# One weight load of a fused attention and mixture kernel, asked for in five pieces of its partitions instead of one

## The chip, the cores and the metric

The kernel runs on one core of one Trainium2 chip. A core has five engines that run side by side: TensorE (PE in the profile, its weight loads PEld), VectorE (DVE), ScalarE (ACT), GpSimd (POOL) and SyncE (SP), and sixteen DMA engines that move data between the main memory and the core's own memories. The metric is the time of one execution in microseconds (us), the median of several.

## What is computed

Sliding-window causal attention over 8 batches, 8 heads, 576 positions and 64 values per head, and behind it a soft mixture of 8 experts with 4 slots each:

```
scores = scale * q @ k.T          # where 0 <= row - column < 64
x = softmax(scores) @ v           # 4608 rows x 512
logits = x @ phi                  # 4608 x 32 slots
slot_input = softmax over rows of logits, transposed, @ x
slot_out[e] = relu(slot_input[e] @ w1[e]) @ w2[e]    # w1: 512 x 1024, w2: 1024 x 512
out = softmax over slots of logits @ slot_out        # 4608 x 512
```

All inputs and the output are float32. The kernel computes in float16; the loads issued from POOL convert on the way.

## The kernel before

The attention runs in 32 steps, one for each batch and pair of heads, in a software pipeline written out by hand: the order of the source is the order on each engine. Step `n` loads inputs for later steps, turns q and k, and does the scores, the maximum, the exponentials and the products of earlier steps. The logits and the slots' sums are folded in by batches. When the last batch is through, the slot inputs `sit` are known; then the experts' two layers run (`first`, L827, and `second`, L851), the result is gathered (`osb`, L880), and the rows of the output are made and written (`cps`, L898 to L905).

The weights are loaded all along from POOL's queue. `worder` lists the loads: the second half of the first matrix of the first weights, the other seven matrices, then the second weights. Of these the first six are whole matrices (`load_w2(e)`, e = 0 to 5), the last two come as halves of their columns: matrix 6 left, matrix 7 left, matrix 6 right, matrix 7 right. `load_w(n)` takes the next n of the list; where it is called (`wslot` and a few calls by hand) fixes their place among POOL's other work. A whole matrix of the second weights is 128 partitions of 8 rows of 512: each partition reads 16 KB in one run and writes 8 KB.

The sixth matrix of the second weights is the last load before POOL does `old_rows` (L515 to L526), which rearranges the sums of the earlier batches; its source order is

```python
    load_w(1)                  # the sixth matrix
    oldr, lgM = old_rows()
    load_w(2)                  # matrix 6 left, matrix 7 left
    ...
    load_w(2)                  # matrix 6 right, matrix 7 right
    scaled(nc.gpsimd, wO, five(olT), 0)      # L787, on POOL
```

The tensor `wO` that `scaled` writes goes into the slot inputs: DVE adds to it at L796 and builds `sit` at L804, which `first` multiplies with the first weights. Matrices six to eight of the second weights lie in a pool that takes the place of the staging buffers of q and k, which are closed by then.

The waits between engines are put in by the framework. For DMA requests from POOL it has eight completion semaphores, which it gives out in turn, in program order. A request that takes a semaphore again gets a wait, on POOL, for the request that had it before, unless POOL has already waited for that one. There are 68 requests from POOL in all. Outputs are requested from SP.

Of the kernel before, what the change touches and what calls it, by code (L numbers as in the profile page):

```python
# [20 lines left out]
def kernel(  # L21
# [10 lines left out]
    nc = tc.nc  # L32

    B, H, S, Dh = q.shape
    D, NSLOT = moe_phi.shape
    E, _, F = moe_w1.shape
# [22 lines left out]
    w2_t = [pwt.tile([128, NFC, D], FP16, name=f"w2_{e}") for e in range(NW2)]  # L59
# [4 lines left out]

    DH = D // 2

    def load_w2(e, d0=0, d1=D):
        src = moe_w2[e].rearrange("(p c) d -> p c d", p=128)
        nc.gpsimd.dma_start(out=w2_t[e][:, :, d0:d1], in_=src[:, :, d0:d1])

    att = ExitStack()
    apsum = ExitStack()
# [63 lines left out]
    for t_, src in reversed(tuple(zip(firsts, (q, k)))):  # L136
        nc.sync.dma_start(out=t_.rearrange("p (h e) -> p h e", h=2),
                          in_=src[0, 0:2].rearrange("h (p r) d -> p h (r d)", r=RQ))
# [370 lines left out]
    def old_rows():  # L509
# [10 lines left out]
        for r in range(4):  # L520
# [4 lines left out]
            if r:  # L525
                nc.gpsimd.tensor_tensor(out=ts[0], in0=ts[0], in1=ts[r], op=ALU.add)  # L526
        return ts[0], wq[:, 8 * w_:8 * w_ + 192]

    NH = 2
    worder = ([(load_w1, 0, 2, 4)] + [(load_w1, e) for e in range(1, E)] + [(load_w2, e) for e in range(E - NH)]  # L530
              + [(load_w2, e, DH * h, DH * h + DH) for h in range(2) for e in range(E - NH, E)])
    worder.reverse()

# [373 lines left out]
    for h in range(2):  # L907
        d0, d1 = DH * h, DH * h + DH
# [39 lines left out]
```

## Time and profile before

| | us |
|---|---|
| median of 3 runs | 192.03 |
| lowest, highest | 191.03, 193.9 |
| the profiled execution, its own time | 193.47 |
| its span, first to last instruction | 191.7 |

| engine | busy us | share of the span |
|---|---|---|
| PE | 152.3 | 79% |
| DVE | 138.4 | 72% |
| ACT | 131.2 | 68% |
| POOL | 130.9 | 68% |

The profile is one execution. The shares are averages over stages with different limits. The page's second part cuts the span into 40 slices of 4.8 us and gives the busy share of each engine in tenths; the sixteen DMA engines are at nine tenths in nearly all of them:

```profile
POOL 8798999997877969989796797966894840000000
DMA  6999999999999999999999999999999999999995
GB/s 145 188 180 184 198 189 182 175 220 178 175 215 181 174 208 183 174 205 194 179 205 195 179 192 212 203 216 215 217 214 212 205 197 164 229 347 367 408 431 250
```

The requests are in the page's sixth part (what, engine, operation, count, KB each, median us from issue to landing). The weights are 13 loads of a matrix or its size and 6 smaller ones:

```profile
w<-in_moe_w_dram POOLq DMA_DIRECT2D x13, 1024.0 KB, 17.7
vr<-in_v_dram POOLq DMA_DIRECT2D x16, 288.0 KB, 14.0
out_dram<-ob SPq DMA_DIRECT2D x2, 2304.0 KB, 7.4
ks<-in_k_dram POOLq DMA_DIRECT2D x15, 288.0 KB, 11.3
qs<-in_q_dram POOLq DMA_DIRECT2D x15, 288.0 KB, 11.8
out_dram<-oh SPq DMA_DIRECT2D x9, 384.0 KB, 4.8
w<-in_moe_w_dram POOLq DMA_DIRECT2D x6, 512.0 KB, 18.9
...
ks<-in_k_dram POOLq DMA_DIRECT2D x1, 144.0 KB, 5.0
qs<-in_q_dram POOLq DMA_DIRECT2D x1, 144.0 KB, 4.9
...
phi_sb<-in_moe_phi_dram POOLq DMA_DIRECT2D x1, 32.0 KB, 9.5
```

A time behind a request is the time until the whole of it has landed, so it holds the queue ahead of it. Waits are put down to the one that ended last.

### The profile page before, as it was taken

The page shows a single profiled execution, that of the slowest core. Times are in us where ns is not written, and L with a number is a line of the kernel's source. Part 1 is how long each engine was busy: PE and PEld are TensorE (multiplying, and loading weights), DVE is VectorE, ACT ScalarE, POOL GpSimd, SP SyncE. Part 2 cuts the span into 40 slices and gives each one's busy share as a digit, 9 for nine tenths or more (in the row PEclk, how much of TensorE's full clock was granted, in tenths as well). Part 3 has the DMA queues.
Part 4 walks back from the last instruction along what each step waited for, and adds up shares of the span by engine and source line. Part 5 has one row for each costly group of instructions (what it writes and reads, how often), then busy time and mean ns, then how long its engine had stood idle before and what let it go on. Part 6 is the DMA issues. An engine that isn't in the chain of part 4 may idle for free.

```text
span 191.7 us, 6887 instructions
## 1 busy us (share of the span) xinstructions
PE 152.3 (79%) x2886; PEld 114.2 (60%) x2886; DVE 138.4 (72%) x306; ACT 131.2 (68%) x255; POOL 130.9 (68%) x257
## 2 busy tenths in 40 slices
PE   5639878897979798988889888989889898689700
PEld 1428777785868587767678676857756245453100
DVE  5794898697888789877969877787675751668420
ACT  5933968878889589889778887969562141677500
POOL 8798999997877969989796797966894840000000
PEclk9855999999999999999999999999999699965555
DMA  6999999999999999999999999999999999999995
GB/s 145 188 180 184 198 189 182 175 220 178 175 215 181 174 208 183 174 205 194 179 205 195 179 192 212 203 216 215 217 214 212 205 197 164 229 347 367 408 431 250
DMA packets 61279, 41.14 MB, mean 215 GB/s; under 512 B 38720, under 2 KB 58944, under 8 KB 59328
## 3 DMA queue, kind: packets, MB, share of 16 engines
q0 software_dynamic: 56384, 30.68, 120.0%
q1 hardware_dynamic: 4864, 10.03, 14.1%
q8 instruction: 22, 0.36, 0.7%
q14 instruction: 9, 0.07, 0.1%
HBM read 61.93 MB, written 9.44 MB: 372 GB/s over the span
## 4 chain that ended last, share of the span: by engine, by line
DVE 30%; PE 25%; DMA 18%; issue 11%; POOL 8%; ACT 5%; DVEq 1%; ACTq 0%; POOLq 0%
DMA w<-in_moe_w_dram 12%; DVE m L309 10%; DVE x_b L363 6%; PE av L353 6%; PE mx L304 3%; PE sc L336 3%; DMA out_dram<-ob 3%; PE sc L333 3%; POOL vr L523 3%; DMA ks<-in_k_dram 3%; PE cp L898 2%; ACT pt L329 2%; PE kb L272 2%; DVE rt L316 2%; DVE rc L362 2%
## 5 line engine op out<-in xcount | busy, mean ns | idle before, releaser
L279 ACT ACTIVATE qz<-qb 64x576 f16<-64x576 f16 x64 | 41.1, 642 | 0.4
L309 DVE TENSOR_REDUCE m<-mx 128x10 f16<-128x960 f32 x32 | 36.8, 1149 | 1.4 <-PE mx L304 1.1
L341 ACT ACTIVATE pt<-sc 128x1024 f16<-128x1024 f32 x29 | 29.7, 1023 | 7.6 <-PE sc L336 6.2
L282 ACT ACTIVATE kT<-kb 128x576 f16<-128x576 f16 x32 | 20.8, 650 | 13.9 <-PE kb L272 13.5
L363 DVE TENSOR_TENSOR x_b<-av,rc 128x640 f16<-128x640 f32 x31 | 25.6, 824 | 1.1
L316 DVE CAST rt<-av 9x128 f16<-9x128 f32 x30 | 8.7, 289 | 17.9 <-PE av L313 17.2
L353 PEld LDWEIGHTS <-pt 128*64 128x64 f16 x576 | 13.2, 110 | 12.0 <-issue 6.2
L304 PE MATMUL mx<-kT,qz 128*64 128x96 f16 x576 | 19.4, 211 | 1.2 <-issue 1.0
L117 POOL DMA_DIRECT2D vr<-in_v_dram x16 | 20.1, 1254 | 0.0
L336 PE MATMUL sc<-qz,kT 128*128 128x128 f16 x232 | 18.6, 222 | 1.7 <-issue 1.7
L333 PE MATMUL sc<-rt,lh 128*128 128x128 f16 x232 | 18.2, 222 | 0.0
L304 PEld LDWEIGHTS <-qz 128*64 128x64 f16 x576 | 15.7, 113 | 3.6 <-issue 3.6
L272 PE MATMUL kb<-ident_h,ki 96*128 96x96 f16 x192 | 14.3, 213 | 4.1 <-POOL ki L108 2.9
L336 PEld LDWEIGHTS <-kT 128*128 128x128 f16 x256 | 16.3, 99 | 2.1 <-issue 2.1
L353 PE MATMUL av<-vs,pt 128*64 128x65 f16 x279 | 13.9, 197 | 4.5 <-ACT pt L329 4.2
L108 POOL COPY ki<-ks 96x384 int32<-96x384 int32 x31 | 15.6, 504 | 1.9 <-DMA ks<-in_k_dram 0.8
L108 POOL COPY qi<-qs 96x384 int32<-96x384 int32 x31 | 15.6, 505 | 0.9 <-DMA qs<-in_q_dram 0.9
L333 PEld LDWEIGHTS <-lh 128*128 128x128 f16 x256 | 15.9, 99 | 0.1
L376 PE MATMUL tx<-ident_h,x_b 128*128 128x128 f16 x160 | 14.4, 219 | 1.6 <-issue 1.4
L353 PE MATMUL av<-vr,pt 128*64 128x65 f16 x279 | 15.4, 198 | 0.2 <-issue 0.2
L272 PEld LDWEIGHTS <-ki 96*128 96x128 f16 x192 | 9.6, 100 | 10.0 <-POOL ki L108 4.4
L287 PE MATMUL mx<-wm,sel 64*128 64x480 f16 x32 | 12.0, 375 | 3.6 <-DVE m L309 2.8
(203 smaller groups left out, 370.5 us busy)
## 6 DMA issues: line engine op xcount, KB each, us to landing
w<-in_moe_w_dram POOLq DMA_DIRECT2D x13, 1024.0 KB, 17.7
vr<-in_v_dram POOLq DMA_DIRECT2D x16, 288.0 KB, 14.0
out_dram<-ob SPq DMA_DIRECT2D x2, 2304.0 KB, 7.4
ks<-in_k_dram POOLq DMA_DIRECT2D x15, 288.0 KB, 11.3
qs<-in_q_dram POOLq DMA_DIRECT2D x15, 288.0 KB, 11.8
out_dram<-oh SPq DMA_DIRECT2D x9, 384.0 KB, 4.8
w<-in_moe_w_dram POOLq DMA_DIRECT2D x6, 512.0 KB, 18.9
out_dram<-ob SPq DMA_DIRECT2D x1, 768.0 KB, 5.3
```

The source lines that it names most:

```text
L108: nc.gpsimd.tensor_copy(out=d_, in_=s_.rearrange("p h r d -> p r h d"))
L117: nc.gpsimd.dma_start(out=vrs[b % 3][:, c0:c1, 0:64], in_=src[:, c0:c1, :])
L272: nc.tensor.transpose(tp[:, j, :], src[:, j].rearrange("p h d -> p (h d)"), ident_h[0:GP, 0:GP])
L279: nc.scalar.activation(dst[r, hl], src[r], AF.Copy, scale=scale)
L282: nc.scalar.activation(kTs[p % NQ][:, 64:64 + S].rearrange("p (g j) -> p g j", j=RQ), ps[:, 0:RQ * GP].rearrange("p (j g) -> p g j", j=RQ) ...
L304: nc.tensor.matmul(mx[64 * t:64 * t + 64, i // 5, 96 * (i % 5):96 * (i % 5) + 96], heads(p, o, 32), kT[:, o:o + 96], start=False, stop=Tru ...
L309: nc.vector.reduce_max(ms[p % 2][:, 0:10].rearrange("p (h c) -> p h c", h=2), mx[:, :, 0:480].rearrange("p h (c x) -> p h c x", x=96), axi ...
L333: nc.tensor.matmul(sc[:, i // 4 - o, 128 * (i % 4):128 * (i % 4) + 128], lh[:, i, :], turned_max(p), start=(i % 4 == 0), stop=False, skip_ ...
L336: nc.tensor.matmul(sc[:, i // 4 - o, 128 * (i % 4):128 * (i % 4) + 128], kTs[p % NQ][:, 64 * i:64 * i + 128], heads(p, 64 * i, 64), start= ...
L341: nc.scalar.activation(pts[p][:, 0:8, :, :], sc[:, :, :].rearrange("p u (c l x) -> p (u c) l x", l=2, x=64), AF.Exp)
L353: nc.tensor.matmul(av[r0:r0 + 64, hl, 65 * (i // 2):65 * (i // 2) + 65], pt[:, i, hl, :], values(b, h, i), start=True, stop=True, skip_gro ...
L363: nc.vector.tensor_tensor(out=x_b[:, :, 128 * hp:128 * hp + 128].rearrange("p c (l d) -> p l c d", l=2), in0=avv[:, :, :, 0:64], in1=rc[:, ...
```

## The change

`load_w2` gets a list of partitions at which a load is cut, and issues one request for each piece. The default is one piece of 128 partitions, as before. The sixth matrix is asked for as partitions 0 to 95 and then four times eight partitions: five requests from POOL at the place of one. All other loads, their order and their places stay.

```diff
-    def load_w2(e, d0=0, d1=D):
+    def load_w2(e, d0=0, d1=D, cuts=(0, 128)):
         src = moe_w2[e].rearrange("(p c) d -> p c d", p=128)
-        nc.gpsimd.dma_start(out=w2_t[e][:, :, d0:d1], in_=src[:, :, d0:d1])
+        for p0, p1 in zip(cuts, cuts[1:]):
+            nc.gpsimd.dma_start(out=w2_t[e][p0:p1, :, d0:d1], in_=src[p0:p1, :, d0:d1])
...
-    worder = ([(load_w1, 0, 2, 4)] + [(load_w1, e) for e in range(1, E)] + [(load_w2, e) for e in range(E - NH)]
+    worder = ([(load_w1, 0, 2, 4)] + [(load_w1, e) for e in range(1, E)] + [(load_w2, e) for e in range(E - NH - 1)]
+              + [(load_w2, E - NH - 1, 0, D, (0, 96, 104, 112, 120, 128))]
               + [(load_w2, e, DH * h, DH * h + DH) for h in range(2) for e in range(E - NH, E)])
```

## The prediction

> **What bounds the kernel now.** I read the page first, for the span and the writes, then the chain of waits, because the change is in a transfer and the chain tells whether transfers set the end.
>
> ```profile
> span 191.7 us, 6887 instructions
> HBM read 61.93 MB, written 9.44 MB: 372 GB/s over the span
> ```
>
> The chain of waits (start, length, what) from the issue of the sixth matrix on:
>
> ```profile
> 131.33 0.50 POOL w L69
> ...
> 131.90 1.70 POOL vr L515 x4
> ...
> 140.97 0.52 POOL vr L526
> 141.49 2.62 POOL w L69 x3
> 144.11 23.64 DMA w<-in_moe_w_dram
> 167.76 0.04 issue
> 167.80 0.43 PE ops L851 x8
> ...
> 174.51 5.34 DMA out_dram<-ob
> ```
>
> The reader is to see three things. The sixth matrix is issued at 131.33, and right behind it on POOL stands `old_rows` (131.90 to 141.49), then the four half loads of the last two matrices. The last half load is under way for 23.64 us, and the last PE block of the second layer starts when it has landed. So the end hangs on the transfer now, not on POOL. But POOL has more to do behind those loads, and what slack it has there I read in its timeline (start, length, engine, line, operation, idle time ahead):
>
> ```profile
> 113.19 0.55 POOL L69 DMA_DIRECT2D w<-in_moe_w_dram  x1
> ...
> 116.11 0.53 POOL L69 DMA_DIRECT2D w<-in_moe_w_dram  x1
> ...
> 120.07 0.53 POOL L69 DMA_DIRECT2D w<-in_moe_w_dram  x1
> ...
> 123.39 0.60 POOL L69 DMA_DIRECT2D w<-in_moe_w_dram  x1
> ...
> 127.87 0.58 POOL L69 DMA_DIRECT2D w<-in_moe_w_dram  x1
> ...
> 131.30 0.53 POOL L69 DMA_DIRECT2D w<-in_moe_w_dram  x1 [1.45 <-DVE xt L383]
> ...
> 141.43 3.56 POOL L69 DMA_DIRECT2D w<-in_moe_w_dram  x4
> 147.38 0.53 POOL L787 TENSOR_TENSOR vr<-vr 128x160 f32<-128x160 f32 x1 [2.39 <-ACT vr L774]
> ```
>
> These are matrices one to six and the four halves. After the halves POOL is idle for 2.39 us, until ACT hands it the factors for L787. So a delay of POOL costs nothing up to 2.4 us and then one for one, as the next rows show.
>
> ```profile
> 147.94 0.76 DVE L796 TENSOR_TENSOR vr<-vr 128x160 f32<-128x160 f32 x1 [0.24 <-POOL vr L787]
> ...
> 150.05 3.73 PE L827 MATMUL hh<-w,sit 128*32 128x512 f16 x48 [0.65 <-DVE sit L804]
> ...
> 162.15 0.40 PE L851 MATMUL ops<-w,hT 128*32 128x256 f16 x8 [0.39 <-DMA w<-in_moe_w_dram]
> ...
> 167.80 0.40 PE L851 MATMUL ops<-w,hT 128*32 128x256 f16 x8 [1.53 <-DMA w<-in_moe_w_dram]
> ```
>
> DVE's L796 waits for POOL's L787, the slots (`sit`) come out of that, and PE's first layer waits for the slots. From there to the end PE waits for weights twice, 0.39 and 1.53 us. If POOL comes late, those 1.92 us are all that can absorb it on PE.
>
> **The change part by part.** *The transfer.* The same bytes go, in five requests instead of one. One request of 128 pieces takes POOL 0.50 to 0.60 us (the rows above), and a half load, with eight times the pieces, 3.56 / 4 = 0.89 us; so the length hardly hangs on the pieces, and I take 0.5 us for each of the five. That is 2.0 us more on POOL, between nothing and 4 x 0.6 = 2.4. Alone it would vanish in the 2.39 us of idle time ahead of L787. The four halves issued 2 us later would find the queue still full, since the last of them lies 23.64 us before it lands.
>
> *The completion semaphores.* This is where the change bites. The framework gives the requests from POOL eight completion semaphores in turn, and a request that takes a semaphore again waits, on POOL, until the request eight before it has landed whole. The page lists 19 + 16 + 16 + 16 + 1 = 68 such requests, so now the last half has number 4 of the turn, the sixth matrix number 8, the first matrix number 3. Such a wait shows as a row of its own when it stands ahead of a request:
>
> ```profile
> L69 POOLq EVENT_SEMAPHORE  x1: 17/17/17, 128.0 to 128.0; - x1
> ```
>
> The row does not name its semaphore, and no request in this trace is held by one, so the price has to come from the landings: issue to landing of matrices one to six, one window for each, in order.
>
> ```profile
> DMA to landing us min/median/max: 18.5/18.5/18.5
> ...
> DMA to landing us min/median/max: 20.8/20.8/20.8
> ...
> DMA to landing us min/median/max: 22.1/22.1/22.1
> ...
> DMA to landing us min/median/max: 23.6/23.6/23.6
> ...
> DMA to landing us min/median/max: 24.1/24.1/24.1
> ...
> DMA to landing us min/median/max: 25.5/25.5/25.5
> ```
>
> With the issue times they land at 131.7, 136.9, 142.2, 147.0, 152.0 and 156.8. Now the halves take numbers 1 to 4, whose last owners are the two requests ahead of matrix one, and matrices one and two: landed by 136.9, before 141.4. With the change the piece of 96 has number 8, the four eights 1 to 4, and the halves 5 to 8. Step by step on POOL: the piece of 96 at 131.3, three eights by 133.4 (matrix one, number 3, has landed at 131.7). The fourth eight needs matrix two, 136.9, and is out at 137.4. What is queued behind it on POOL is `old_rows`, which starts at 137.4 instead of 131.9 and ends at 141.5 + 5.5 = 147.0. First half: needs matrix three (142.2), free, 147.0 to 147.9. Second: matrix four (147.0), free, to 148.8. Third: matrix five, 152.0, out at 152.9. Fourth: the piece of 96. A whole matrix takes 156.8 - 152.0 = 4.8 us behind the fifth; three quarters of it, 3.6, give 155.6; out at 156.5. If the 96 partitions lie unevenly on the sixteen engines it is between half a matrix (154.4) and a whole one (156.8), so 1.2 us either way.
>
> So L787 starts at 156.5 instead of 147.4: **9.1 us later, 7.9 to 10.3**. SP issues nothing before the outputs and is not passed. The transfers themselves keep their end: the fourth half is in the queue at 156.5, before the third has been moved, and lands at about 167.8 as now.
>
> *From there to the end.* PE loses the two waits: its last block of the second layer moves from 167.80 by 9.1 - 1.9 = 7.2 us, to 175.0, and no longer waits for any weights. The first output moves by 9.1 - 0.4 = 8.7 us, from 163.8 to 172.5. The outputs, and the windows (stretch, length, busy time of PE, PEld, DVE, ACT, POOL, clock, DMA share, GB/s):
>
> ```profile
> L905 SPq DMA_DIRECT2D out_dram<-oh x11: 369/436/1027, 163.8 to 172.9; - x11
> L905 SPq DMA_DIRECT2D out_dram<-ob x3: 332/344/448, 174.5 to 183.4; - x3
> ...
> DMA to landing us min/median/max: 4.1/4.9/7.4
> ```
>
> ```profile
> 160.00:161.00 1.00, 1.00 (x25) 0.77 (x27) 0.51 (x3) 0.00 (x0) 0.00 (x0) 1.00 1.37 187
> 162.00:163.00 1.00, 0.40 (x8) 0.26 (x8) 0.00 (x0) 0.37 (x1) 0.00 (x0) 1.00 0.72 95
> ...
> 168.00:190.80 22.80, 12.41 (x45) 5.29 (x37) 11.16 (x19) 10.37 (x19) 0.00 (x0) 0.52 0.97 375
> 180.00:185.00 5.00, 1.43 (x3) 0.29 (x2) 3.37 (x5) 2.43 (x4) 0.00 (x0) 0.50 1.03 435
> ```
>
> The last output is issued at 183.4 and lands 7.4 later, at 190.8; 0.9 us follow. Three readings of the output stage, all starting at 172.5. At the best rate of the trace, 435 GB/s, 9.44 MB take 21.7 us: end 195.1, +3.4. At the mean rate after the weights, 375 GB/s, 25.2 us: 198.6, +6.9. If everything behind the last PE block keeps its distance: +7.2. I take **+6.5**, nearer to the last two, since they come from this very stage, and a little under them, since the transfers no longer share with weights. Span 198.2; the profiled execution took 193.47 for a span of 191.7, so 200.0 on that count. That execution stands 1.4 us over the median of 192.03, to which I add the same 6.5: **198.5 us**.
>
> The clock of PE after the longer gap I cost at nothing, because the first layer starts cold already, as the windows show:
>
> ```profile
> 150.00:152.00 2.00, 1.95 (x23) 0.69 (x26) 1.90 (x7) 0.00 (x0) 1.45 (x5) 0.56 1.09 189
> ```
>
> The Trainium skill's page "TensorE: Matmul & The Clock Gate", Part 1, says that after an idle window PE runs at half clock for about 3.4 us of sustained work; against the 2 us at 0.56 seen here that would make the first layer an estimated 0.8 us longer and the sum 199.3.
>
> **The rivals.** *Not slower: the balance of the DMA engines decides.* The rate of the weights falls from 187 to 95 GB/s between 160 and 163, before the last has landed at 167.8: about half of the sixteen engines have then run dry. If the four eights fall on the early ones, the late ones carry six of eight shares of this matrix and finish a quarter of 4.8 us = 1.2 us earlier; the wait of 1.53 before the last PE block is the most that this can give. That makes 192.0 - 1.2 = 190.8, or 193.2 if the eights fall on the late ones. For it speaks that the transfer ends the chain now; against it, that it decides only if POOL loses under 2.4 us, so if the waits for matrices two, five and six are not made at all, or are for something landed long before. Chance 0.13. The page "DMA: Bandwidth & Descriptors" of the Trainium skill ("Why a DMA increments its semaphore by 16 and not by 1") has eight partitions on eight engines, taken in turn from a cursor; by that, two shares would come to each engine, and this rival would give 192.0. No row here shows which engine carries what.
>
> *The whole delay reaches the end.* If the output stage is bound by evictions that start 9.1 us later and the two PE waits were hiding something else, the end moves by 9.1: 201.1. For it: DVE and ACT show half of the stage busy, and the last output waits for a buffer (174.51, 5.34 us in the chain). Against: the 1.92 us of PE's waiting are plainly there to be lost. Chance 0.15.
>
> *The outputs run at their best rate throughout*: +3.4, 195.4. For it: no weights beside them. Against: the clock is 0.5 there and evictions feed them. Chance 0.05.
>
> **How the numbers follow.** The forecast proper, with POOL held by the semaphores and +4 to +8.5 at the end, has 0.67. Likeliest time 198.5. The range goes down to the best output rate, 195.4, and up to the whole delay with a little of the landing's 1.2 us: 201.8. What is left out is mainly the rival that is not slower. 2% of 192 is 3.8 us, about what a measurement of this kernel tells from no change; slower by more than that: 0.67 + 0.15 and part of the 0.05, so 0.84; within: 0.14; faster by over 2% would need more than the 1.53 us that the last wait holds: 0.02.
>
> **What would show it.** In the changed kernel's POOL timeline the fourth eight should start near 136.9, behind a wait of about 3.5 us; `old_rows` should end near 147; the four halves should come apart, the last two near 152.0 and 155.6; L787 near 156.5 with no wait for ACT. PE should show an idle stretch of some 9 us before L827 and no wait for weights after it. I am wrong if L787 stays near 147.4 (then the semaphores do not bind), or if L787 is late and the end is not (then the output stage had more room than the rows show).

## The result, and the profile after

| | us |
|---|---|
| median before, in the same comparison | 192.05 |
| median after | 201.94 |
| ratio, after to before | 1.049, 95% interval 1.042 to 1.057 |
| profiled execution after: its time, its span | 201.81, 200.0 |

The ratio leaves out two of the six executions after (204.84 and 203.68), which were in a slower state that some executions show, so it stands for 192.05 x 1.049 = 201.5 us and not quite for the median. The change makes the kernel slower by about 9.5 us. The forecast was 198.5, in a range up to 201.8: right in direction and mechanism, short by 3 us in size. The 201.5 lies just inside that range, the median just above it.

The timeline of POOL after the change (start, length, engine, line, operation, idle time ahead and what ended it; `load_w2` is now at L70, `scaled` at L789):

```profile
130.29 2.05 POOL L70 DMA_DIRECT2D w<-in_moe_w_dram  x4 [1.22 <-PE qb L273]
136.08 0.50 POOL L70 DMA_DIRECT2D w<-in_moe_w_dram  x1 [3.74 <-DVE x_b L364]
136.64 1.69 POOL L516 TENSOR_TENSOR vr<-acc,vr 128x128 f32<-128x128 f32 x4
...
145.72 0.52 POOL L527 TENSOR_TENSOR vr<-vr 128x160 f32<-128x160 f32 x1
146.44 1.86 POOL L70 DMA_DIRECT2D w<-in_moe_w_dram  x2 [0.20 <-issue]
152.55 0.87 POOL L70 DMA_DIRECT2D w<-in_moe_w_dram  x1 [4.26 <-DMA w<-in_moe_w_dram]
155.84 0.87 POOL L70 DMA_DIRECT2D w<-in_moe_w_dram  x1 [2.42 <-DMA w<-in_moe_w_dram]
156.73 0.54 POOL L789 TENSOR_TENSOR vr<-vr 128x160 f32<-128x160 f32 x1
```

The piece of 96 and three eights go out together, and then POOL stands still for 3.74 us before the fourth eight. `old_rows` runs behind it, the first two halves follow at once, and the last two come out one by one, 4.26 and 2.42 us later. The wait of 2.39 us for ACT ahead of `scaled` is gone. The name on the first of the three waits misleads: the DVE instruction only happened to end last before the wait did. What was waited for is read from landings. The rows are issue to landing for matrix two (issued at 115.88), matrix five (127.09) and the piece of 96 (130.29), one window each:

```profile
DMA to landing us min/median/max: 19.9/19.9/19.9
...
DMA to landing us min/median/max: 25.2/25.2/25.2
...
DMA to landing us min/median/max: 25.3/25.3/25.3
```

They land at 135.8, 152.3 and 155.6, each about 0.25 us ahead of a request at 136.08, 152.55 and 155.84. These are the owners of the semaphores that the prediction named.

The chain of waits shows what then carries the delay to the end (start, length, what):

```profile
127.09 25.18 DMA w<-in_moe_w_dram
152.27 0.28 issue
152.55 0.87 POOL w L70
...
155.85 0.87 POOL w L70
...
156.73 0.55 POOL vr L789
...
157.30 0.77 DVE vr L798
...
159.42 4.62 PE hh L829 x46
...
170.31 1.44 PE ops L853 x32
...
171.78 0.38 ACT osb L882
...
182.98 5.12 DMA out_dram<-ob
```

The transfer in the chain is no longer the last half load, which PE needed. It is matrix five, which nobody needed yet: it only had to land to give its semaphore back. Behind it come POOL, DVE and PE in a row, then the gathering of the result (`osb`) and the outputs. PE's timeline shows the hole, and that the weights are there when PE comes for them:

```profile
159.42 4.62 PE L829 MATMUL hh<-w,sit 128*32 128x512 f16 x48 [10.87 <-DVE sit L806]
...
175.05 0.62 PE L853 MATMUL ops<-w,hT 128*32 128x256 f16 x16
```

PE idles for 10.87 us, and its last block of the second layer runs in one piece with no wait for weights. Two runs of eight matmuls were parted by 1.53 us of waiting before.

### The profile page after: what moved, and what is told of

It is laid out like the page before. It is cut to its first block, busy times and chain, and to the rows that moved or that the text cites. A ratio compares the mean times of both kernels' runs of the same rounds, so it can differ in the third digit from the quotient of the medians.

```text
span 200.0 us, 6893 instructions
## 1 busy us (share of the span) xinstructions
PE 153.8 (77%) x2886; PEld 114.8 (57%) x2886; DVE 138.2 (69%) x306; ACT 131.2 (66%) x255; POOL 133.0 (66%) x261
## 3 DMA queue, kind: packets, MB, share of 16 engines
HBM read 61.93 MB, written 9.44 MB: 357 GB/s over the span
## 4 chain that ended last, share of the span: by engine, by line
PE 33%; DVE 21%; DMA 18%; issue 13%; ACT 8%; POOL 2%; DVEq 0%; ACTq 0%; POOLq 0%
DMA w<-in_moe_w_dram 13%; DVE m L310 7%; PE av L354 5%; PE mx L305 4%; PE sc L337 4%; DVE x_b L364 4%; PE sc L334 4%; PE cp L900 3%; PE kb L273 3%; PE hh L829 3%; DMA out_dram<-ob 3%; ACT pt L330 3%; DMA ks<-in_k_dram 2%; PE ops L853 2%; ACT oh L903 1%
## 5 line engine op out<-in xcount | busy, mean ns | idle before, releaser
L317 DVE CAST rt<-av 9x128 f16<-9x128 f32 x30 | 8.7, 289 | 16.3 <-PE av L314 14.7
L337 PEld LDWEIGHTS <-kT 128*128 128x128 f16 x256 | 16.3, 99 | 2.3 <-issue 2.3
L70 POOL DMA_DIRECT2D w<-in_moe_w_dram x14 | 8.9, 640 | 11.8 <-DMA w<-in_moe_w_dram 6.7
L334 PEld LDWEIGHTS <-lh 128*128 128x128 f16 x256 | 15.9, 99 | 0.1
L273 PE MATMUL qb<-ident_h,qi 96*128 96x96 f16 x192 | 14.5, 215 | 1.1 <-POOL qi L109 0.8
```

The costliest lines, as they stand in the source:

```text
L273: nc.tensor.transpose(tp[:, j, :], src[:, j].rearrange("p h d -> p (h d)"), ident_h[0:GP, 0:GP])
L334: nc.tensor.matmul(sc[:, i // 4 - o, 128 * (i % 4):128 * (i % 4) + 128], lh[:, i, :], turned_max(p), start=(i % 4 == 0), stop=False, skip_ ...
L337: nc.tensor.matmul(sc[:, i // 4 - o, 128 * (i % 4):128 * (i % 4) + 128], kTs[p % NQ][:, 64 * i:64 * i + 128], heads(p, 64 * i, 64), start= ...
```

## The experiments

The theory: the five requests cost nothing as transfers. They move the turn of the eight semaphores by four, so that POOL waits in its own queue for matrices two and five and for the piece of 96, and comes late to L789. The rivals: cutting the transfer costs by itself; the eights load the DMA engines unevenly; transfers sent late are part of the loss. Each run was timed against the kernel before on the same chip.

**Two, three and four requests.** Only the number of requests and their sizes change.

```diff
-              + [(load_w2, E - NH - 1, 0, D, (0, 96, 104, 112, 120, 128))]
+              + [(load_w2, E - NH - 1, 0, D, (0, 96, 128))]            # two
+              + [(load_w2, E - NH - 1, 0, D, (0, 96, 112, 128))]       # three
+              + [(load_w2, E - NH - 1, 0, D, (0, 64, 96, 112, 128))]   # four
```

> The sixth matrix in two requests (96 and 32 partitions). Theory, semaphores: one added request moves the turn by one; the halves then wait for the request ahead of matrix one and matrices one, two and three, landed by 142.2, so POOL never stands still for a semaphore; POOL's 0.5 us more is hidden in its idle time; L787 stays at 147.4 and the time at 192, ratio 0.99 to 1.01. Rival, cutting the transfer costs in itself, evenly by request: a quarter of the loss measured with four added requests (9.4 us), so +2.4 us, ratio 1.012, and L787 late or the weights landing later.

> Three requests (96, 16, 16 partitions). Semaphores: the halves wait for matrices one, two, three and four; the fourth goes out near 147.0 and POOL is free at 147.9, so L787 starts about 0.5 us later than before and the end moves by as much; ratio 0.995 to 1.01. Even cost by request: half of 9.4 us, +4.7 us, ratio 1.025.

> Four requests (64, 32, 16, 16 partitions). Semaphores: pieces need nothing that has not landed; the halves wait for matrices two, three, four and five, so the third goes out at 147.0 and the fourth at 152.0; POOL is free at 152.9, L787 at 152.9 instead of 147.4 (+5.5), the first output 5 us later, the end 4 to 5 us later, ratio 1.02 to 1.03. Even cost by request: three quarters of 9.4 us, +7 us, ratio 1.037, L787 near 154.3.

Measured: 0.998 (0.994 to 1.003), 0.997 (0.993 to 1.002) and 1.022 (1.013 to 1.031). The loss does not grow evenly with the requests. It is nothing for one and for two added, 2.2% for three and 4.9% for the change's four. The POOL waits for weights on the page of waits of two (first fence; it has none, so its wait ahead of `scaled` is shown), three and four requests:

```profile
POOL vr L789 <- ACT vr L776: 1.9, 1, 1.9
```

```profile
POOL vr L789 <- ACT vr L776: 1.1, 1, 1.1
POOL w L70 <- DMA w<-in_moe_w_dram: 0.6, 1, 0.6
```

```profile
POOL w L70 <- DMA w<-in_moe_w_dram: 6.1, 2, 4.0
```

The columns are waiter, releaser, total, times, longest. With two requests POOL still waits 1.9 us for ACT ahead of `scaled`; 0.5 us of the idle time has been used. With three (the profile is of an execution of 193.51 us, over the median of 192.23) the first semaphore wait appears, 0.6 us, and 1.1 us of idle time are left, so I had the wait right and its effect wrong: I expected L789 0.5 us late, and the idle time covered it. With four, 6.1 us of waiting are more than it can cover. All three ratios lie in the ranges expected from the semaphores. The times of L789 do not all: with four requests it starts at 150.87 against 152.9 expected. A profile is one execution, and its clock times stand 1 to 2 us off those expected in several runs here, so I compare waits and ratios.

**Five requests with whole sixteens.** The same count, and pieces of a multiple of sixteen partitions, meant to load the sixteen DMA engines alike: `(0, 64, 80, 96, 112, 128)`.

> Five requests as in the change, but of 64, 16, 16, 16, 16 partitions. Semaphores: the same count of requests, so the same waits; the first piece is half a matrix instead of three quarters, so the last half goes out near 154.4 instead of 155.6 and L787 comes near 155.4; ratio 1.04 to 1.05. Rival, the four eights load the same DMA engines and that is the loss: with sixteens every engine has the same share, so the time comes back to before, ratio 1.00 to 1.01.

Measured: 1.036 (1.025 to 1.047). The loss stays, so the rival falls as the main cause. POOL comes to L789 at 153.71, 3.0 us earlier than after the change. Of these, 1.9 are there already at the wait for matrix five, which is the same in both (150.62 here, 152.55 after the change). The other 1.1 are the effect of the smaller piece, as expected: the last half load waits for half a matrix here instead of three quarters of one. The interval of the ratio overlaps with that of the change, so the times alone do not show the difference; the timeline does.

```profile
150.62 0.88 POOL L70 DMA_DIRECT2D w<-in_moe_w_dram  x1 [2.65 <-DMA w<-in_moe_w_dram]
152.82 0.87 POOL L70 DMA_DIRECT2D w<-in_moe_w_dram  x1 [1.32 <-DMA w<-in_moe_w_dram]
153.71 0.54 POOL L789 TENSOR_TENSOR vr<-vr 128x160 f32<-128x160 f32 x1
```

**The matrix whole, and four tiny requests.** Nothing is cut; four requests that write 256 bytes each into unused columns are put behind the whole matrix.

```diff
     load_w(1)
+    for i in range(4):
+        tin = vrs[M % 3].rearrange("p c x -> p (c x)")[0:16, 2944 + 8 * i:2952 + 8 * i]
+        nc.gpsimd.dma_start(out=tin, in_=moe_phi[0:16, 8 * i:8 * i + 8])
     oldr, lgM = old_rows()
```

> The sixth matrix in one request as before, and behind it four requests of 16 partitions by 8 values each, which nothing uses. Semaphores: same waits as the change, and the last half waits for the whole matrix (156.8): L787 near 157.9, ratio 1.045 to 1.06. Rival, the cut transfer is the cause: nothing is cut, the tiny requests cost POOL 2 us, which its idle time covers; ratio 1.00 to 1.01.

Measured: 1.044 (1.036 to 1.052), just under the range expected; POOL comes to `scaled` at 155.99 instead of 157.9. Four requests that carry next to nothing cost as much as the cut. That leaves the cutting, and the load that the pieces put on the DMA engines, no part of the loss that these intervals can show. This trace also puts the right name to the first wait (the timeline of POOL):

```profile
131.48 1.50 POOL L656 DMA_DIRECT2D vr<-in_moe_phi_dram  x3 [0.72 <-PE av L313]
134.53 0.49 POOL L656 DMA_DIRECT2D vr<-in_moe_phi_dram  x1 [1.55 <-DMA w<-in_moe_w_dram]
```

The fourth tiny request waits for weights that it has nothing to do with.

**The change, with POOL's remaining work ahead of the last two halves.** The requests are those of the change; only their place in POOL's queue differs.

```diff
-    load_w(2)
     scaled(nc.gpsimd, wO, five(olT), 0)
...
     fr_place(L)
+    load_w(2)
```

> The changed kernel's five requests, but POOL does its remaining work (L787, the copies for the output, the last placements) ahead of the last two half loads. Semaphores: the fourth eight is still held until matrix two has landed, so the first two halves end near 148.9 and L787 starts there, 1.5 us later than before; the last two halves go out near 158, when their semaphores are long free, and land near 168; ratio 1.00 to 1.012. Rival, five requests cost by themselves: the loss stays, ratio 1.04 and more.

Measured: 1.001 (0.997 to 1.006). The whole loss is gone. POOL reaches `scaled` at 147.12, and the last two halves go out when nobody stands behind them:

```profile
134.83 0.50 POOL L70 DMA_DIRECT2D w<-in_moe_w_dram  x1 [2.89 <-DVE rc L363]
...
145.23 1.87 POOL L70 DMA_DIRECT2D w<-in_moe_w_dram  x2 [0.18 <-issue]
147.12 0.54 POOL L789 TENSOR_TENSOR vr<-vr 128x160 f32<-128x160 f32 x1
...
155.60 1.81 POOL L70 DMA_DIRECT2D w<-in_moe_w_dram  x2
```

The wait of 2.89 us ahead of the fourth eight is still there and costs nothing that can be measured. So the loss came from the two later waits, which stood in front of `scaled`. (The 1.81 us that POOL takes to issue the two halves have moved behind `scaled` too; that is part of what pays for the first wait.)

**The kernel before, with POOL kept busy.** All loads as before; 17 copies stand ahead of `scaled`.

```diff
     load_w(2)
+    for _ in range(17):
+        nc.gpsimd.tensor_copy(out=ct4[0:32].bitcast(I32), in_=ctr[0:32].bitcast(I32))
     scaled(nc.gpsimd, wO, five(olT), 0)
```

> The kernel before, all loads as they were, with 17 copies on POOL between the last half load and L787 (the first of the copies for the output, done 17 times over; 0.69 us each by the rows of before, 11.7 us from 145.0). Theory, the loss is POOL's lateness at L787 and nothing in the transfers: L787 near 156.7, first output near 173, last landing 26 us after it, ratio 1.04 to 1.055 as the change. Rival, transfers sent late or cut are part of the loss: less than the change, ratio 1.02 to 1.035.

Measured: 1.049 (1.043 to 1.056), as the change. A late POOL is enough, with every transfer issued as before.

**The change, with PE kept busy.** `fill(3)` ahead of the first layer becomes `fill(40)`.

> The changed kernel with 40 filling matmuls instead of 3 ahead of the first layer, so that PE does not stand idle while it waits for the slots. If the clock after the gap costs the first layer its 0.9 us (48 matmuls in 4.62 us against 3.73), they take 3.8 us or less and the end comes about 0.9 us earlier than in the change (span near 199); if not, they stay near 4.6 us.

One execution, 201.26 us, span 199.5. The windows of this run (first fence: while PE fills, and the first layer) and of the change (second fence) give the clock in the third column from the right:

```profile
148.00:158.00 10.00, 10.00 (x40) 4.10 (x38) 1.39 (x4) 0.00 (x0) 4.58 (x7) 0.85 1.24 198
158.50:162.00 3.50, 3.11 (x48) 1.19 (x48) 2.56 (x9) 0.61 (x2) 2.59 (x7) 1.00 1.38 189
```

```profile
150.00:159.00 9.00, 0.00 (x0) 0.00 (x0) 1.52 (x5) 0.00 (x0) 3.93 (x6) 0.50 1.38 188
159.40:162.00 2.60, 2.58 (x28) 0.91 (x32) 2.18 (x7) 0.00 (x0) 1.97 (x6) 0.50 1.38 193
```

The 48 matmuls take 3.18 us at clock 1.00 instead of 4.62, of which the first 2.6 us are at 0.50. That is the shorter first layer that I expected. But the first output comes only 0.4 us sooner behind `scaled` (15.9 us against 16.3), since the next PE instruction now waits 0.98 us for ACT. The span is 0.5 us shorter than after the change, and POOL came to `scaled` 0.8 us earlier (155.90 against 156.73), so the end gained nothing that one execution can tell.

**Wide rows.** On the kernel before, six row blocks of the second group are written once at full width instead of in two halves.

```diff
-        for j0, j1 in ((0, 3), (3, 6)):
-            cps(1, j0, j1, d0, d1)
-    cps(1, 6, 9)
+    cps(1, 0, 3)
+    cps(1, 3, 9)
```

> The kernel before, with the second group's first six row blocks made and written once at full width behind both halves (3 and then 6 blocks), instead of twice at half width; the loads stay. In every run so far the last landing comes 26.1 to 26.9 us behind the first output. If the DMA engines bind that stage, at 339 GB/s for the 1 KB rows of the half-width pieces and over 420 for the wide ones, 1.57 MB gain 1.57/0.339 - 1.57/0.42 = 0.9 us, less what the engines stand idle between the halves: ratio 0.993 to 1.0, last landing 25.3 to 26.2 us behind the first output. If evictions bind it, the same number of elements leaves PSUM and the time stays or grows: ratio 1.0 to 1.01.

Measured: 1.002 (0.999 to 1.006). The gain expected did not come, and the last landing is 26.7 us behind the first output. Wide rows do move faster (408 GB/s in the second window, 345 in the same window before), but the DMA engines now run short ahead of them (share 0.82 in the first):

```profile
169.00:172.00 3.00, 3.00 (x9) 1.24 (x9) 2.90 (x6) 2.28 (x6) 0.00 (x0) 0.50 0.82 271
172.00:175.00 3.00, 3.00 (x9) 1.05 (x7) 1.70 (x3) 1.24 (x2) 0.00 (x0) 0.50 1.08 408
```

In the kernel before the same two windows have shares of 1.03 and 1.04. So this run does not decide whether transfers or evictions set the length of the output stage: the time fits the rival of evictions, and the gap in the transfers would hide a gain as well. No version tried beats the kernel before.

## Why the prediction was right, and where it was short

**The semaphores held, step by step.** The eight-in-turn reckoning gave the fourth eight at 136.9, the halves at 147.0, 152.0 and 155.6, and L787 at 156.5. Measured were 136.08, 146.44, 152.55, 155.84 and 156.73. The four tiny requests show that the count of requests does it, and the change with POOL's rest first shows which waits do it.

How closely the times agree is in part luck. The execution after stood 1.0 us ahead at the sixth matrix (130.29 against 131.30), and matrix five was under way for 25.2 us instead of 24.1; the two nearly cancel. Counted from the sixth matrix, POOL came to `scaled` 26.4 us later, against 16.1 before. That is a loss of 10.4 us, just above the 7.9 to 10.3 forecast.

One reading of mine did not hold: that a semaphore wait ahead of a request shows as a row of its own. After the change three requests are held, and the line still has one such row, in the same place as before, during the issue of matrix five:

```profile
L70 POOLq EVENT_SEMAPHORE  x1: 17/17/17, 127.2 to 127.2; - x1
```

The waits show as idle time of POOL alone.

**The slack of 2.39 us held.** Runs with one and with two added requests lie within it and cost nothing.

**Transfers keep their end: held.** The last half load, issued at 155.84, was under way for 12.6 us and landed at 168.4; the forecast was 167.8. PE never waited for weights after the change, and POOL's copies alone give the same loss.

**The sum was short at the end.** The step that failed is the term for the output stage. I set the first output at 172.5 and let 9.44 MB take 25.2 us at the mean rate, and 0.9 behind them: a span to 198.6, of which I then took 0.4 off because no weights would be under way beside the outputs. Measured: first output at 173.0 (0.5 later) and 27.0 us from there to the span's end (0.9 more). 0.5 + 0.9 + 0.4 = 1.8 us, the difference of the spans 200.0 and 198.2. So the 25.2 us measured 26.1: the last output landed at 199.1.

Behind this stands what the end hangs on. My third reading, +7.2, took the last PE block as the measure, so that PE's two waits for weights absorb 1.9 us of the delay. That block did move as forecast, from 167.80 to 175.05, 7.25 us against 7.2. But the chain of waits after the change does not pass through it. The chain passes through the block at 170.31, whose weights had landed, and goes from there to the first outputs. So the first output is the measure, and it moved by 9.2 us (163.8 to 173.0). Behind it the stage has nearly one length, as the profiles show (wide rows is left out, since it writes its outputs otherwise):

| kernel | POOL at `scaled` | first output issued | span | span less first output |
|---|---|---|---|---|
| before | 147.38 | 163.8 | 191.7 | 27.9 |
| two requests | 146.27 | 162.5 | 189.6 | 27.1 |
| three requests | 148.81 | 164.7 | 191.7 | 27.0 |
| five, rest first | 147.12 | 163.4 | 190.5 | 27.1 |
| four requests | 150.87 | 167.7 | 194.7 | 27.0 |
| five sixteens | 153.71 | 169.6 | 196.7 | 27.1 |
| POOL kept busy | 155.38 | 172.0 | 199.0 | 27.0 |
| whole and four tiny | 155.99 | 172.2 | 199.2 | 27.0 |
| the change | 156.73 | 173.0 | 200.0 | 27.0 |
| the change, PE kept busy | 155.90 | 171.8 | 199.5 | 27.7 |

First outputs follow `scaled` at 15.9 to 16.8 us, and the span's end follows them at 27.0 or 27.1 in eight of the ten rows. In the profile of before it is 27.9. There the last PE block waited for weights until 167.80, 4.0 us behind the first output; with two requests it waited until 165.60, 3.1 us behind. That would account for the 0.9 us, though no run isolates it. The 27.7 with PE kept busy, where no block waited for weights, stays unexplained. So against the one profile of before, 0.9 us of the delay are absorbed. Against the runs that lose nothing, none is: from `scaled` to the end it is 43.3 us with two requests, 43.4 with POOL's rest first and 43.3 after the change. The outcome was nearest to the rival in which the whole delay reaches the end (201.1, chance 0.15). The best-rate reading (195.4), the low end of my range, would need a stage 4.4 us shorter than the change shows; no row comes near it.

**The rest is the execution.** Another 1.6 us of the 3.4 between 198.5 and 201.94 has nothing to do with the mechanism. I added a difference of spans to a median. The profiled execution before stood 1.4 us over its median, the one after (201.81) 0.1 under its own.

**The clock of PE** I cost at nothing, and that held. After the change the clock is 0.50 at first and the 48 matmuls take 4.62 us, against 3.73 before. But the longer gap is not what they pay for. With two requests PE idles for only 0.47 us ahead of them, the clock is 0.50 from 149 to 152 as well, and they take as long:

```profile
148.95 4.58 PE L829 MATMUL hh<-w,sit 128*32 128x512 f16 x48 [0.47 <-DVE sit L806]
```

In the run with sixteens, behind 6.75 us of idle time, they take 4.15 us. So the length differs from execution to execution whatever the gap, and the expectation that the gap costs 0.9 us was wrong. The Trainium skill's page "TensorE: Matmul & The Clock Gate", Part 1, has half clock for about 3.4 us of sustained work after an idle window. The 0.50 after the gap of 10.87 us agrees with it; the 0.8 us estimated from it does not show as a price of the change.

**The rival of balanced engines** falls as an account of this change: POOL does lose more than 2.4 us, and the loss stays with whole sixteens and with nothing cut. What the eights alone would gain or lose was not tested cleanly. In the run with POOL's rest first the waits cost nothing, and its 1.001 (0.997 to 1.006) speaks against the gain (190.8 would be 0.994) and hardly against the loss (193.2 would be 1.006); but its last halves also go out later.

## What to carry to other kernels

With this framework a DMA request from POOL takes a completion semaphore as well as a place in a queue; before adding one, count which earlier request must land to free the semaphore, for this request and for the next eight behind it. The price is paid by what stands behind the waiting request on its engine, so put such requests behind the work that others wait for. Read the slack ahead of the first instruction that others need: a delay inside it is free, and a delay beyond it counted one for one here, because the stage that ends the kernel has nearly one length. When you ask what a delay is worth at the end, follow the chain as it will be after the change: a wait that ends the chain now absorbs nothing if the chain no longer passes through it.

## What the runs showed of the hardware that was not expected

Eight partitions take nearly as long as sixteen. After the change the piece of 96 lands at 155.6, and by issue and landing the first, third and fourth eight land at 156.1, 157.2 and 157.9: about 0.57 us for each eight. In the run with sixteens the first and the fourth sixteen land at 153.2 and 155.1, three steps of 0.63. As an estimate, a whole matrix of 128 partitions, spread evenly over sixteen engines, is eight partitions to an engine in 4.8 us, or 0.6 for each. So the steps are those that one late engine would show if it carried a share of every eight. No run here names the engines.

The Trainium skill's page "DMA: Bandwidth & Descriptors" ("Why a DMA increments its semaphore by 16 and not by 1") has eights on eight engines from a cursor that moves on, as the prediction used it; the steps do not fit with that. The exception that it gives in the same place, partitions spread over the engines from the first one on, would fit.

SP's own issue of an output is not of one length. After the change the first request of 384 KB, at 174.3, takes SP 0.38 us, and the last, at 181.8, takes 1.09 us. By issue and landing, two smaller outputs were under way at the first, and some four at the last, since each then took 4.4 us to land and one went out about every 1.1 us. That the outputs under way lengthen the issue is my reading; no run tests it. The row holds these requests and two smaller ones (0.37 and 0.41 us):

```profile
L907 SPq DMA_DIRECT2D out_dram<-oh x11: 369/744/1091, 173.0 to 181.8; - x11
```
